# Last-layer weights converted from doubles beside the products that precede their use, earlier splits for the first expert, and four smaller edits

## The chip, the cores and the metric

One core of one Trainium2 chip runs the kernel. The metric is device time in microseconds (us), the median of the runs shown. Engines are named as in the profile: PE (TensorE matmul), PEld (its weight loads), DVE (VectorE), ACT (ScalarE), POOL (GpSimd) and SP (SyncE, which issues most DMAs). Lines such as L298 are lines of the kernel before.

## The reference

Three layers in a row, all in float32 at the ends: linear attention with a normalised output, a mixture of experts with one expert per token and a capacity, and a maxout layer.

```python
kv = einsum('bhsd,bhse->bhde', k, v); out = einsum('bhsd,bhde->bhse', q, kv)      # B 4, H 8, S 576, D 64
x = (out / sqrt(mean(out * out, -1) + 1e-6) * g_norm) as (2304, 512)
expert = argmax(x @ w_gate); gate = softmax weight of that expert                 # 8 experts
y[i] = gate * (relu(x[i] @ w1[e]) @ w2[e])       # w1 512x1024, w2 1024x512, first `capacity` tokens of each
h = maximum(maximum(y @ m1, y @ m2), y @ m3); result = h @ w_out                  # m 512x768, w_out 768x512
```

The four matrices of the maxout layer (`m1`, `m2`, `m3`, `w_out`) arrive as 64-bit doubles; everything else is 32-bit.

## The kernel before

**Stages.** The attention runs batch by batch (four of them). Each batch's tokens are normalised, routed and scattered to DRAM by expert; the tokens of the fullest expert are also picked straight from SBUF for the first expert's product. Eight experts follow (`r` from 0 to 7, the order ranked by load), then the maxout layer in six blocks of 384 tokens (`j` from 0 to 5).

**Splits.** Each big product is made of three passes in a rounded format: the operands are split into a high and a low part, and high x high, high x low and low x high are summed (`mm3`, L765 to L767). A weight tile of 128x512 therefore costs two instructions: the high part on ACT (L297) and the low part on DVE (L298). `split_next` does the next tile of one fixed stream: 16 tiles for each expert, then 18 of the three maxout matrices, then 6 of `w_out`. It is fed by `raw` tiles in a ring of four, loaded by SP (`raw_dma`), each reused when its two splits are done. Activations are split the same way: `h` (L788 on ACT, L789 on DVE), `xt` (L678, L679), `g` (L1099, L1100).

**An expert.** `gemm1_f` runs eight times (`f`), each giving 128 rows of `h`; `gemm2_dc` runs four times (`dc`) and reads all eight `h`. Between them the written order puts splits, gathers, the next expert's transposes and `dbl_step`s.

**Doubles.** `dbl_step` turns one 128x256 piece of a double matrix into float32: SP loads it, ACT rounds its two words (L912, L913), DVE does three integer steps (L914, L915, L917), POOL multiplies and adds (L918, L919), and ACT's queue stores the piece to DRAM. There are 48 pieces (36 of the three matrices, 12 of `w_out`), placed in experts 1 to 7 by the tables `DBL1` (after which `f`) and `DBL2` (how many after each `dc`).

**Maxout.** For each of six column blocks `c`, PE makes three products `pa` (12 groups of `mm3`, one bank of PSUM each). ACT copies the first (L1096), DVE takes the maximum with the second and the third (L1097, L1098), ACT and DVE split the result (L1099, L1100). Then three output tiles `pz` sum over the six blocks (L1109 to L1111). PSUM has six banks here (`psb`, bufs=6): block `c+2` writes over the banks of block `c`.

**Order.** Nothing reorders the program: each engine executes its queue in the order in which the program is written (`manual_schedule`), and waits at the head of the queue hold all that stands behind.

Of the kernel before, what the change touches and what calls it, by code (L numbers as in the profile page):

```python
# [40 lines left out]
def kernel(  # L41
# [21 lines left out]
    ct = dram.tile([NT, 3], F32, name="ct")  # L63

    doubles = []
    if m2w1.dtype == mybir.dt.int64:
        d64 = [m2w1, m2w2, m2w3, m2wo]
        m2w1, m2w2, m2w3 = (dram.tile([DM, F2], F32, name=f"m2w{a}") for a in range(3))
        m2wo = dram.tile([F2, DM], F32, name="m2wo")
        for cb in range(F2 // 256):  # L70
            for a, dst in enumerate([m2w1, m2w2, m2w3]):
                for rb in range(NDC):
                    doubles.append((d64[a], dst, rb, cb))
        for rb in range(NC2):
            for cb in range(DM // 256):
                doubles.append((d64[3], m2wo, rb, cb))
    ND = len(doubles)
# [155 lines left out]
    sp, act = ENG.SP, ENG.Activation  # L233
    NRAW = NE * 8 + 12
    NW = 20
# [12 lines left out]
    def raw_dma(i):  # L248
# [16 lines left out]
        if j < 9:  # L265
# [3 lines left out]
        j -= 9  # L269
        return nc.sync.dma_start(raw.rearrange("p (c f) -> p c f", c=2),  # L270
                                 m2wo[j * 256:(j + 1) * 256, :].rearrange("(c p) f -> p c f", p=128))

# [7 lines left out]

    def split_next(n=1, eng=None):
        for _ in range(n):
            i, half = divmod(stream[0], 2)
            stream[0] += 1
            if i >= NRAW:
                continue
            raw = raws[i]
            t_ = wtile(2 * i + half)
            wt[2 * i + half] = t_
            if i < NE * 8 + 9:  # L290
                src = raw.rearrange("p (c f) -> p c f", c=4)[:, :, half * 128:(half + 1) * 128]
                hi, lo = t_[:, 0], t_[:, 1]
            else:
                src = raw[:, half * 512:(half + 1) * 512]
                hi = t_[:, 0].rearrange("p c f -> p (c f)")
                lo = t_[:, 1].rearrange("p c f -> p (c f)")
            nc.scalar.activation(out=hi, in_=src, func=AF.Copy)  # L297
            (eng or nc.vector).tensor_tensor(out=lo, in0=src, in1=hi.bitcast(F32), op=ALU.subtract)  # L298
            if half == 1:
                raw_upto(i + 5)  # L300
# [101 lines left out]
    def out_rest(b, qT):  # L402
        po = ps_o.tile([128, 512], F32, tag="po", name=f"po{b}r")[:, 0:4 * LW].rearrange("p (j c) -> p j c", c=LW)
        sq = sa.tile([128, H, 2, D], F32, tag="sq", bufs=2, name=f"sq{b}r")[:, 0:2].rearrange("p a b d -> p (a b) d")
# [58 lines left out]
    def stats_steps(b, t0, t1, r_):  # L463
# [9 lines left out]
        yield  # L473
        nc.scalar.activation(out=sr, in_=ms, func=AF.Sqrt)
        yield
# [426 lines left out]
    def dbl_round(i):  # L902

        if i < ND:
            t_ = dt_[i]
            w_ = dpool[0].tile([128, 256], F32, tag="dw", bufs=6, name=f"dw{i}")
            dt_[i, "w"] = w_
            lo, hi = t_[:, :, 0], t_[:, :, 1]  # L910
            wi = w_.bitcast(I32)
            nc.scalar.activation(out=w_, in_=hi.bitcast(F32), func=AF.Copy, scale=2.0 ** -112)  # L912
            nc.scalar.activation(out=lo.bitcast(F32), in_=lo.bitcast(U32), func=AF.Copy, scale=2.0 ** -52)  # L913
            nc.vector.tensor_scalar(out=wi, in0=wi, scalar1=3, scalar2=None, op0=ALU.logical_shift_left)  # L914
            nc.vector.scalar_tensor_tensor(out=wi, in0=hi, scalar=-2 ** 31, in1=wi,  # L915
                                           op0=ALU.bitwise_and, op1=ALU.bitwise_or)
            nc.vector.tensor_scalar(out=hi, in0=wi, scalar1=-2 ** 23, scalar2=None, op0=ALU.bitwise_and)  # L917
            nc.gpsimd.tensor_tensor(out=lo.bitcast(F32), in0=hi.bitcast(F32), in1=lo.bitcast(F32), op=ALU.mult)  # L918
            nc.gpsimd.tensor_tensor(out=w_, in0=lo.bitcast(F32), in1=w_, op=ALU.add)  # L919

# [107 lines left out]

    DBL1 = [(), (3, 5), (3, 5), (1, 3, 5), (1, 4), (1, 4), (1, 4), (1, 3, 5, 7)]
    DBL2 = [(0, 0, 0, 0), (1, 1, 1, 2), (1, 2, 1, 2), (1, 2, 1, 2), (1, 1, 1, 2)] + [(1, 1, 1, 1)] * 2 + [(2, 2, 0, 0)]  # L1030
    for r in range(NE):
# [10 lines left out]
        if r == NE - 1:  # L1042
            ct_load()
        for f in range(NFC):
            gemm1_f(r, f)
            if r == 0:
                for _ in range(9 if f == 0 else 6):
                    next(rk_gen, None)
                if f == 3:
# [32 lines left out]
    for j in range(NYB):  # L1082
        h2 = []
        for c in range(NC2):
# [36 lines left out]
    with tc.If(flag):  # L1121
        spill(ctx, tc, dict(
            er_f=er_f, nr_f=nr_f, mr_f=mr_f, trir=trir, capf=capf, e2304=e2304, slot=slot, ident=ident, g2=g2,
            xs=xs, ct=ct, w1=w1, w2=w2, m2w=m2w, m2wo=m2wo, out=out))


def spill(ctx, tc, a):
# [3 lines left out]
    with ExitStack() as st:  # L1131
# [164 lines left out]
```

## Time and profile before

| what | value |
|---|---|
| median of 3 runs | 647.64 us (646.8 to 650.21) |
| the profiled execution, its own time | 650.49 us |
| its span | 648.6 us, granted clock 0.982 |
| PE busy | 619.0 us, 95% |
| DVE, ACT, POOL busy | 338.0, 274.0, 196.5 us |

The span runs from the first to the last profiled instruction; 1.9 us of the execution's own time lie around it. Attention lasts to about 88 us, the experts to about 337, the maxout layer to the end.

### The profile page before, as it was taken

How to read it: one execution, taken by the hardware profiler on the slowest of the kernel's cores; microseconds unless marked ns; L12 is line 12 of the kernel's file. 1: busy time of each engine (PE TensorE's matmuls, PEld its weight loads, DVE VectorE, ACT ScalarE, POOL GpSimd, SP SyncE). 2: the span in 40 equal slices, each digit the busy share in tenths (PEclk: the TensorE clock that was granted, in tenths of full speed). 3: DMA queues.
4: the chain of work that ended last, by engine and by line, in shares of the span. 5: the costliest groups of instructions: out<-in, count | busy, mean ns of one | idle time of the engine just before them, and what ended most of it. 6: DMA issues, size and time to landing. Idle time of an engine off the chain costs nothing.

```text
span 648.6 us, 11278 instructions
## 1 busy us (share of the span) xinstructions
PE 619.0 (95%) x4113; PEld 593.8 (92%) x4113; DVE 338.0 (52%) x718; ACT 274.0 (42%) x629; POOL 196.5 (30%) x278
## 2 busy tenths in 40 slices
PE   8898988999999999999999999999999999999992
PEld 8788888999998989999999989989989989989992
DVE  2546867886889888888985322222322222221220
ACT  1655864856575857576753221121121121121110
POOL 3247643122858585857530010010010010001001
PEclk9978998999999999999999999999999999999997
DMA  8999347866888788888962000000000000000000
GB/s 226 282 297 297 122 164 236 256 234 214 246 249 276 235 264 254 259 251 255 275 184 65 1 34 16 1 33 17 1 33 17 0 17 33 0 17 33 1 18 35
DMA packets 81373, 88.35 MB, mean 136 GB/s; under 512 B 15017, under 2 KB 70825, under 8 KB 81314
## 3 DMA queue, kind: packets, MB, share of 16 engines
q1 hardware_dynamic: 68448, 66.64, 35.5%
q0 software_dynamic: 5952, 14.65, 6.5%
q10 hardware_dynamic: 6914, 6.30, 2.8%
q8 instruction: 34, 0.56, 0.4%
q14 instruction: 25, 0.20, 0.1%
HBM read 71.80 MB, written 15.76 MB: 135 GB/s over the span
## 4 chain that ended last, share of the span: by engine, by line
PE 63%; DVE 9%; DMA 4%; issue 3%; ACT 2%; ACTq 0%; POOL 0%; SPq 0%; DVEq 0%; POOLq 0%
PE pa L767 12%; PE pa L766 12%; PE pa L765 12%; PE py L766 4%; DVE w L298 4%; PE py L767 4%; PE py L765 4%; PE pz L1110 4%; PE pz L1109 4%; PE pz L1111 4%; DVE h L789 2%; DMA d<-in_moe_w_dram 2%; PE ph L767 2%; PE ph L766 2%; PE ph L765 2%
## 5 line engine op out<-in xcount | busy, mean ns | idle before, releaser
L766 PE MATMUL pa<-ys,w 128*128 128x384 f32 x432 | 144.3, 334 | 0.0
L765 PE MATMUL pa<-ys,w 128*128 128x384 f32 x432 | 144.3, 334 | 0.0
L767 PE MATMUL pa<-ys,w 128*128 128x384 f32 x432 | 144.3, 334 | 0.0
L298 DVE TENSOR_TENSOR w<-raw,w 128x512 fp32r<-128x512 f32 x152 | 114.6, 783 | 26.7 <-ACT w L297 23.1
L1114 POOL DMA_INDIRECT out_dram<-o,ctab x18 | 17.5, 973 | 286.9 <-ACT o L1113 276.7
L1097 DVE TENSOR_TENSOR m<-pa,m 128x384 f32<-128x384 f32 x36 | 20.1, 558 | 137.6 <-PE pa L767 137.6
L297 ACT ACTIVATE w<-raw 128x512 fp32r<-128x512 f32 x152 | 89.5, 624 | 4.8 <-DMA raw<-in_moe_w_dram 4.8
L766 PE MATMUL py<-h,w 128*128 128x324 f32 (+7 forms) x256 | 81.4, 318 | 7.2 <-DVE h L789 7.2
L1099 ACT ACTIVATE g<-m 128x384 fp32r<-128x384 f32 x36 | 18.9, 526 | 150.0 <-DVE m L1098 150.0
L766 PEld LDWEIGHTS pa<-ys,w 128*128 128x128 f32 x432 | 81.1, 188 | 0.2
L765 PEld LDWEIGHTS pa<-ys,w 128*128 128x128 f32 x432 | 81.1, 188 | 0.2
L767 PEld LDWEIGHTS pa<-ys,w 128*128 128x128 f32 x432 | 81.1, 188 | 0.0
L765 PE MATMUL py<-h,w 128*128 128x324 f32 (+7 forms) x256 | 80.2, 313 | 0.0
L767 PE MATMUL ph<-xt,w 128*128 128x324 f32 (+7 forms) x256 | 79.6, 311 | 0.5 <-DVE w L298 0.5
L765 PE MATMUL ph<-xt,w 128*128 128x324 f32 (+7 forms) x256 | 79.3, 310 | 0.6 <-ACT xt L667 0.6
L767 PE MATMUL py<-h,w 128*128 128x324 f32 (+7 forms) x256 | 79.8, 312 | 0.0
L766 PE MATMUL ph<-xt,w 128*128 128x324 f32 (+7 forms) x256 | 79.4, 310 | 0.2 <-DVE xt L668 0.2
L766 PEld LDWEIGHTS py<-h,w 128*128 128x128 f32 x256 | 48.8, 191 | 10.8 <-DVE h L789 10.6
L918 POOL TENSOR_TENSOR d<-d 128x256 f32<-128x256 f32 x48 | 30.7, 640 | 75.5 <-issue 18.2
L765 PEld LDWEIGHTS ph<-xt,w 128*128 128x128 f32 x256 | 48.3, 189 | 0.8 <-ACT xt L667 0.8
L767 PEld LDWEIGHTS ph<-xt,w 128*128 128x128 f32 x256 | 48.3, 189 | 0.8 <-DVE w L298 0.8
L765 PEld LDWEIGHTS py<-h,w 128*128 128x128 f32 x256 | 48.9, 191 | 0.0
(247 smaller groups left out, 1034.1 us busy)
## 6 DMA issues: line engine op xcount, KB each, us to landing
raw<-in_moe_w_dram SPq DMA_DIRECT2D x64, 512.0 KB, 5.4
d<-in_moe_w_dram SPq DMA_DIRECT2D x36, 256.0 KB, 5.2
m2w<-dw ACTq DMA_DIRECT2D x36, 128.0 KB, 4.5
raw<-m2w SPq DMA_DIRECT2D x9, 512.0 KB, 4.6
k<-in_k_dram SPq DMA_DIRECT2D x8, 512.0 KB, 8.7
v<-in_v_dram SPq DMA_DIRECT2D x8, 512.0 KB, 9.2
q<-in_q_dram SPq DMA_DIRECT2D x8, 512.0 KB, 8.5
d<-in_moe_w_out_dram SPq DMA_DIRECT2D x12, 256.0 KB, 5.2
```

Source lines behind the costliest of these rows:

```text
L297: nc.scalar.activation(out=hi, in_=src, func=AF.Copy)
L298: (eng or nc.vector).tensor_tensor(out=lo, in0=src, in1=hi.bitcast(F32), op=ALU.subtract)
L765: nc.tensor.matmul(po, lhi, rhi, start=first, stop=False)
L766: nc.tensor.matmul(po, lhi, rlo, start=False, stop=False)
L767: nc.tensor.matmul(po, llo, rhi, start=False, stop=last)
L918: nc.gpsimd.tensor_tensor(out=lo.bitcast(F32), in0=hi.bitcast(F32), in1=lo.bitcast(F32), op=ALU.mult)
L1097: nc.vector.tensor_tensor(out=m_, in0=pa[1][:, :YB], in1=m_, op=ALU.max)
L1099: nc.scalar.activation(out=t_[:, 0], in_=m_, func=AF.Copy)
L1109: nc.tensor.matmul(po, h_[:, 0], w_[:, 0], start=c == 0, stop=False)
L1110: nc.tensor.matmul(po, h_[:, 0], w_[:, 1], start=False, stop=False)
L1111: nc.tensor.matmul(po, h_[:, 1], w_[:, 0], start=False, stop=c == NC2 - 1)
L1114: nc.gpsimd.indirect_dma_start(out=out, out_offset=IndirectOffsetOnAxis(ap=ctab[:, jt, 0:1].bitcast(I32), axis=0), in_=o_, in_offset=None)
```

## The change

- The 12 `w_out` pieces leave the `dbl_step` tables. Instead six 128x512 pieces of doubles are loaded as `raw` tiles and converted by the same seven operations (now a function, `to_float32`) inside `split_next`, in the first block of the maxout layer. The converted piece is split as before, and both parts are stored to DRAM for a fallback path that this input does not take.
- `DBL1` and `DBL2` spread the remaining 36 pieces anew.
- In expert 0 the splits stand ahead of the products: four before the first, two before each of the next four, one after each of the last two.
- The root of the sums of squares is taken on ACT from the sums themselves (scale and bias inside the instruction).
- In the last batch DVE scales three of five row sets instead of two, and does so ahead of the positions' cast; ACT scales two instead of three; one group of 128x128 products that keep PE busy is three long instead of four.
- A work tile of the rest rows gets a buffer of its own.

```diff
-    NRAW = NE * 8 + 12
+    NRAW = NE * 8 + 9 + NC2
...
-        return nc.sync.dma_start(raw.rearrange("p (c f) -> p c f", c=2),
-                                 m2wo[j * 256:(j + 1) * 256, :].rearrange("(c p) f -> p c f", p=128))
+        return nc.sync.dma_start(raw.bitcast(I32), m2wo[j * 128:(j + 1) * 128, :].bitcast(I32))
...
+    def to_float32(lo, hi, w_):
+        wi = w_.bitcast(I32)
+        nc.scalar.activation(out=w_, in_=hi.bitcast(F32), func=AF.Copy, scale=2.0 ** -112)
+        nc.scalar.activation(out=lo.bitcast(F32), in_=lo.bitcast(U32), func=AF.Copy, scale=2.0 ** -52)
+        nc.vector.tensor_scalar(out=wi, in0=wi, scalar1=3, scalar2=None, op0=ALU.logical_shift_left)
+        nc.vector.scalar_tensor_tensor(out=wi, in0=hi, scalar=-2 ** 31, in1=wi,
+                                       op0=ALU.bitwise_and, op1=ALU.bitwise_or)
+        nc.vector.tensor_scalar(out=hi, in0=wi, scalar1=-2 ** 23, scalar2=None, op0=ALU.bitwise_and)
+        nc.gpsimd.tensor_tensor(out=lo.bitcast(F32), in0=hi.bitcast(F32), in1=lo.bitcast(F32), op=ALU.mult)
+        nc.gpsimd.tensor_tensor(out=w_, in0=lo.bitcast(F32), in1=w_, op=ALU.add)
...
             else:
-                src = raw[:, half * 512:(half + 1) * 512]
...
+                src = xgs[0].tile([128, H, D], F32, tag="xn", name=f"wd{i}").rearrange("p h d -> p (h d)")
+                words = raw.bitcast(I32).rearrange("p (f c) -> p f c", c=2)
+                to_float32(words[:, :, 0], words[:, :, 1], src)
             nc.scalar.activation(out=hi, in_=src, func=AF.Copy)
...
+            if i >= NE * 8 + 9:
+                c0 = (i - NE * 8 - 9) * 128
+                nc.sync.dma_start(m2wos[c0:c0 + 128].rearrange("p s f -> p (s f)"),
+                                  t_.bitcast(F32).rearrange("p s c f -> p (s c f)"))
...
-        nc.scalar.activation(out=sr, in_=ms, func=AF.Sqrt)
+        nc.scalar.activation(out=sr, in_=s_, func=AF.Sqrt, scale=1.0 / D, bias=eps)
...
-    for s in SORD[:3]:
+    for s in SORD[:2]:
         normalise(b, s, nc.scalar)
-    keep_warm(ps_o.tile([128, 512], F32, tag="po", name="warm6"), 4)
+    keep_warm(ps_o.tile([128, 512], F32, tag="po", name="warm6"), 3)
...
     own(b)
+    for s in SORD[2:]:
+        normalise(b, s, nc.vector)
     send(b)
-    for s in SORD[3:]:
-        normalise(b, s, nc.vector)
...
-    DBL1 = [(), (3, 5), (3, 5), (1, 3, 5), (1, 4), (1, 4), (1, 4), (1, 3, 5, 7)]
-    DBL2 = [(0, 0, 0, 0), (1, 1, 1, 2), (1, 2, 1, 2), (1, 2, 1, 2), (1, 1, 1, 2)] + [(1, 1, 1, 1)] * 2 + [(2, 2, 0, 0)]
+    DBL1 = [(), (3, 5, 7), (1, 3, 5, 7), (1, 3, 5, 7), (3, 7), (7,), (), (1, 3, 5)]
+    DBL2 = [(0,) * 4] + [(1,) * 4] * 3 + [(1,) * 4, (1, 1, 1, 0), (1, 1, 1, 0), (0,) * 4]
...
         for f in range(NFC):
+            if r == 0:
+                split_next(4 if f == 0 else 2 if f < 5 else 0)
             gemm1_f(r, f)
...
-            split_next(1 if r else 2 if f < 6 else 0)
+            split_next(1 if r or f > 5 else 0)
...
             if j == 0:
-                split_next(2)
+                split_next(2 if c < 2 else 1)
```

**ACT in the first maxout block, column blocks 1 to 3.** Before (`raw` to `w` is a split; `m`, `g` the maximum and its split):

```order
L1099 ACTIVATE g_4865<-m_4864 128x384
L297 ACTIVATE w_4910<-raw_4734 128x512
L297 ACTIVATE w_4913<-raw_4734 128x512
L1096 ACTIVATE m_4916<-pa_4871 128x384
L1099 ACTIVATE g_4917<-m_4916 128x384
L297 ACTIVATE w_4962<-raw_4779 128x512
L297 ACTIVATE w_4965<-raw_4779 128x512
L1096 ACTIVATE m_4968<-pa_4923 128x384
```

Of the change (`wd` is the float32 that DVE and POOL complete; the L312 row reads it):

```order
L1110 ACTIVATE g_4729<-m_4728 128x384
L283 ACTIVATE wd_4775<-raw_4598 128x512
L284 ACTIVATE raw_4598<-raw_4598 128x512
L312 ACTIVATE w_4774<-wd_4775 128x512
L283 ACTIVATE wd_4789<-raw_4641 128x512
L284 ACTIVATE raw_4641<-raw_4641 128x512
L312 ACTIVATE w_4788<-wd_4789 128x512
L1107 ACTIVATE m_4802<-pa_4735 128x384
L1110 ACTIVATE g_4803<-m_4802 128x384
L283 ACTIVATE wd_4849<-raw_4675 128x512
L284 ACTIVATE raw_4675<-raw_4675 128x512
L312 ACTIVATE w_4848<-wd_4849 128x512
```

Two conversions now stand between the `g` of block 0 and the `m` of block 1, and one ahead of the `m` of each later block.

**DVE in expert 0, up to the first `h`.** Before, and then of the change:

```order
L1023 CAST po_i<-po_f 128x4
L789 SCALAR_TENSOR_TENSOR h_1369<-ph_1356,h_1369 128x324
L808 COPY cnt<-pc 128x8
L811 SCALAR_TENSOR_TENSOR key<-cnt,key_199 128x8
L813 TENSOR_TENSOR gt<-key 128x64
```

```order
L1032 CAST po_i<-po_f 128x4
L313 TENSOR_TENSOR w_1350<-raw_701,w_1350 128x512
L313 TENSOR_TENSOR w_1353<-raw_701,w_1353 128x512
L313 TENSOR_TENSOR w_1358<-raw_703,w_1358 128x512
L313 TENSOR_TENSOR w_1361<-raw_703,w_1361 128x512
L810 SCALAR_TENSOR_TENSOR h_1379<-ph_1366,h_1379 128x324
```

Four splits moved ahead of the first `h`; what stood between later `h` moved up with them.

**DVE in expert 7, around the last two `h`.** Before, and then of the change:

```order
L914 TENSOR_SCALAR dw_4601<-dw_4601 128x256
L915 SCALAR_TENSOR_TENSOR dw_4601<-d_4436,dw_4601 128x256
L917 TENSOR_SCALAR d_4436<-dw_4601 128x256
L789 SCALAR_TENSOR_TENSOR h_4622<-ph_4609,h_4622 128x284
L298 TENSOR_TENSOR w_4625<-raw_4433,w_4625 128x512
L789 SCALAR_TENSOR_TENSOR h_4641<-ph_4628,h_4641 128x284
```

```order
L313 TENSOR_TENSOR w_4486<-raw_4312,w_4486 128x512
L810 SCALAR_TENSOR_TENSOR h_4505<-ph_4492,h_4505 128x284
L313 TENSOR_TENSOR w_4508<-raw_4355,w_4508 128x512
L810 SCALAR_TENSOR_TENSOR h_4524<-ph_4511,h_4524 128x284
```

The rounds of doubles between the `h` are gone there.

## Rows read from the trace of the kernel before

**Rows 1.** The page, part 1: busy time of each engine.

```profile
PE 619.0 (95%) x4113; PEld 593.8 (92%) x4113; DVE 338.0 (52%) x718; ACT 274.0 (42%) x629; POOL 196.5 (30%) x278
```

**Rows 2.** Page and lines by form: all experts, expert 0, expert 3 (busy, mean | idle before).

```profile
L766 PE MATMUL py<-h,w 128*128 128x324 f32 (+7 forms) x256 | 81.4, 318 | 7.2 <-DVE h L789 7.2
...
L766 PE MATMUL py<-h,w 128*128 128x324 f32 x32 | 10.9, 342 | 2.1 <-DVE h L789 2.1
...
L766 PE MATMUL py<-h,w 128*128 128x330 f32 x32 | 10.2, 319 | 1.6 <-DVE h L789 1.6
```

**Rows 3.** Windows: start:end, length, busy of the engines, PEclk, DMA share, GB/s.

```profile
200.00:210.00 10.00, 8.45 (x55) 7.90 (x53) 9.72 (x19) 3.88 (x9) 8.97 (x11) 1.00 0.97 295
344.00:357.00 13.00, 13.00 (x77) 13.00 (x76) 6.00 (x11) 4.35 (x9) 0.00 (x0) 1.00 0.03 11
```

**Rows 4.** Timeline of DVE, maxout block 0 (start, us, instruction, idle before).

```profile
349.78 0.56 DVE L1098 TENSOR_TENSOR m<-pa,m 128x384 f32<-128x384 f32 x1 [1.45 <-PE pa L767]
350.94 0.56 DVE L1100 TENSOR_TENSOR g<-m,g 128x384 fp32r<-128x384 f32 x1 [0.59 <-ACT g L1099]
...
356.02 0.56 DVE L1098 TENSOR_TENSOR m<-pa,m 128x384 f32<-128x384 f32 x1 [1.45 <-PE pa L767]
```

**Rows 5.** Timeline of ACT, maxout block 0.

```profile
344.13 0.53 ACT L1099 ACTIVATE g<-m 128x384 fp32r<-128x384 f32 x1 [2.72 <-DVE m L1098]
344.56 1.14 ACT L297 ACTIVATE w<-raw 128x512 fp32r<-128x512 f32 x2
345.62 0.49 ACT L1096 ACTIVATE m<-pa 128x384 f32<-128x384 f32 x1
350.38 0.53 ACT L1099 ACTIVATE g<-m 128x384 fp32r<-128x384 f32 x1 [4.26 <-DVE m L1098]
```

**Rows 6.** Timeline of DVE, a split and one round of doubles in expert 2.

```profile
159.90 0.69 DVE L298 TENSOR_TENSOR w<-raw,w 128x512 fp32r<-128x512 f32 x1
160.50 0.29 DVE L914 TENSOR_SCALAR dw<-dw 128x256 int32<-128x256 int32 x1
...
161.56 0.29 DVE L914 TENSOR_SCALAR dw<-dw 128x256 int32<-128x256 int32 x1
```

**Rows 7.** Timeline of POOL: one round's second operation, and a whole round.

```profile
304.30 1.09 POOL L919 TENSOR_TENSOR dw<-d,dw 128x256 f32<-128x256 f32 x1
...
307.13 0.61 POOL L918 TENSOR_TENSOR d<-d 128x256 f32<-128x256 f32 x1 [1.75 <-ACT xt L678]
307.82 0.75 POOL L919 TENSOR_TENSOR dw<-d,dw 128x256 f32<-128x256 f32 x1
```

**Rows 8.** Lines by form: a scaling of 512 columns in attention, on POOL.

```profile
L516 POOL TENSOR_TENSOR orow<-ohl,rnorm 128x512 f32<-128x512 f32 x12 | 12.1, 1033 | 0.0
```

**Rows 9.** Timeline of PE, maxout block 0: the first output tile's sixteenth product.

```profile
378.03 0.40 PE L1109 MATMUL pz<-w,g 128*128 128x512 f32 x1
```

**Rows 10.** Timeline of PE in expert 0, around its two waits.

```profile
107.81 0.42 PE L766 MATMUL py<-h,w 128*128 128x324 f32 x1 [1.16 <-DVE h L789]
...
109.42 0.54 PE L766 MATMUL py<-h,w 128*128 128x324 f32 x1 [0.90 <-DVE h L789]
...
110.29 0.47 PE L766 MATMUL py<-h,w 128*128 128x324 f32 x1
```

**Rows 11.** Windows: the stretch after those waits.

```profile
109.00:113.00 4.00, 3.58 (x14) 3.58 (x15) 0.77 (x2) 1.35 (x5) 0.00 (x0) 0.57 0.88 260
```

**Rows 12.** Timeline of DVE in expert 0: the first and the last `h`.

```profile
93.90 0.50 DVE L789 SCALAR_TENSOR_TENSOR h<-ph,h 128x324 fp32r<-128x324 f32 x1 [2.59 <-ACT h L788]
...
108.88 0.89 DVE L789 SCALAR_TENSOR_TENSOR h<-ph,h 128x324 fp32r<-128x324 f32 x2
```

**Rows 13.** Timeline of PE, end of attention: dummies, routing.

```profile
79.88 1.09 PE L331 MATMUL warm<-ident 128*128 128x128 f32 x8
80.81 0.18 PE L531 MATMUL pp<-ohsum,ones 128*128 128x40 bf16 x1
```

More of the change, by code (lines that the diff above doesn't have):

```diff
@@ L66 @@
     if m2w1.dtype == mybir.dt.int64:
-        d64 = [m2w1, m2w2, m2w3, m2wo]
+        d64 = [m2w1, m2w2, m2w3]
         m2w1, m2w2, m2w3 = (dram.tile([DM, F2], F32, name=f"m2w{a}") for a in range(3))
-        m2wo = dram.tile([F2, DM], F32, name="m2wo")
+        m2wos = dram.tile([F2, 2, DM], F32, name="m2wos")
         for cb in range(F2 // 256):
@@ L73 @@
                     doubles.append((d64[a], dst, rb, cb))
-        for rb in range(NC2):
-            for cb in range(DM // 256):
-                doubles.append((d64[3], m2wo, rb, cb))
     ND = len(doubles)
@@ L279, in raw_upto, with split_next @@
             issued[0] += 1
-    def split_next(n=1, eng=None):
+    def to_float32(lo, hi, w_):
[8 more added lines that the diff above has]
+        nc.gpsimd.tensor_tensor(out=w_, in0=lo.bitcast(F32), in1=w_, op=ALU.add)
+    def split_next(n=1):
         for _ in range(n):
-            i, half = divmod(stream[0], 2)
+            t = stream[0]
             stream[0] += 1
-            if i >= NRAW:
+            if t >= NT1 + 18 + NC2:
                 continue
+            i = t // 2 if t < NT1 + 18 else NE * 8 + 9 + t - NT1 - 18
             raw = raws[i]
-            t_ = wtile(2 * i + half)
-            wt[2 * i + half] = t_
+            t_ = wtile(t)
+            wt[t] = t_
             if i < NE * 8 + 9:
+                half = t % 2
                 src = raw.rearrange("p (c f) -> p c f", c=4)[:, :, half * 128:(half + 1) * 128]
@@ L293, in split_next @@
             else:
-                src = raw[:, half * 512:(half + 1) * 512]
-                hi = t_[:, 0].rearrange("p c f -> p (c f)")
-                lo = t_[:, 1].rearrange("p c f -> p (c f)")
-            nc.scalar.activation(out=hi, in_=src, func=AF.Copy)
-            (eng or nc.vector).tensor_tensor(out=lo, in0=src, in1=hi.bitcast(F32), op=ALU.subtract)
+                half = 1
+                hi, lo = (t_[:, x].rearrange("p c f -> p (c f)") for x in range(2))
+                src = xgs[0].tile([128, H, D], F32, tag="xn", name=f"wd{i}").rearrange("p h d -> p (h d)")
+                words = raw.bitcast(I32).rearrange("p (f c) -> p f c", c=2)
+                to_float32(words[:, :, 0], words[:, :, 1], src)
+            nc.scalar.activation(out=hi, in_=src, func=AF.Copy)
+            nc.vector.tensor_tensor(out=lo, in0=src, in1=hi.bitcast(F32), op=ALU.subtract)
+            if i >= NE * 8 + 9:
+                c0 = (i - NE * 8 - 9) * 128
+                nc.sync.dma_start(m2wos[c0:c0 + 128].rearrange("p s f -> p (s f)"),
+                                  t_.bitcast(F32).rearrange("p s c f -> p (s c f)"))
             if half == 1:
@@ L322 @@
         nc.vector.memset(ss[i][D:128, 0, :], 1.0)
+    eps = sl_.tile([128, 1], F32, name="eps")
+    nc.vector.memset(eps, EPS)
     ohsum = sl_.tile([128, B + 1, NE], BF16, name="ohsum")
@@ L403, in out_rest @@
         po = ps_o.tile([128, 512], F32, tag="po", name=f"po{b}r")[:, 0:4 * LW].rearrange("p (j c) -> p j c", c=LW)
-        sq = sa.tile([128, H, 2, D], F32, tag="sq", bufs=2, name=f"sq{b}r")[:, 0:2].rearrange("p a b d -> p (a b) d")
+        sq = sa.tile([128, 4, D], F32, tag="sqr", bufs=1, name=f"sq{b}r")
         for h in range(H):
@@ L909, in dbl_round @@
             dt_[i, "w"] = w_
[L910 to L919, printed above, removed]
+            to_float32(t_[:, :, 0], t_[:, :, 1], w_)
     def dbl_store(i):
@@ L1123 @@
             er_f=er_f, nr_f=nr_f, mr_f=mr_f, trir=trir, capf=capf, e2304=e2304, slot=slot, ident=ident, g2=g2,
-            xs=xs, ct=ct, w1=w1, w2=w2, m2w=m2w, m2wo=m2wo, out=out))
+            xs=xs, ct=ct, w1=w1, w2=w2, m2w=m2w, m2wos=m2wos, out=out))
 def spill(ctx, tc, a):
@@ L1191, in spill @@
         wo = wpool.tile([128, NC2, DM], F32, name="sp_wo")
-        nc.sync.dma_start(wo, a["m2wo"].rearrange("(c p) f -> p c f", p=128))
+        wl = wpool.tile([128, NC2, DM], F32, name="sp_wl")
+        for i, w_ in enumerate((wo, wl)):
+            nc.sync.dma_start(w_, a["m2wos"].rearrange("(c p) s f -> s p c f", p=128)[i])
+        V.tensor_tensor(out=wo, in0=wo, in1=wl, op=ALU.add)
         def ps(nm):
```

## The prediction

> **What bounds the kernel now.** I read the page's busy times first: PE is busy 95% of the span, 619.0 of 648.6 us, and no other engine is near it [rows 1]. So the product stream is the path, and a change can win only what PE loses. Next, where it loses it. The grouped waits of PE on the second layer's products name DVE's low half of `h`, 7.2 us in all: 2.1 in expert 0, 5.1 in experts 1 to 7, none of them with more than expert 3's 1.6 [rows 2]. The windows tell why: around expert 3's waits DVE is busy 9.72 of 10 us and POOL 8.97 [rows 3]. DVE carries the weight splits, the `h` and the rounds of doubles, and falls behind. In the maxout layer it is the other way round: in 344 to 357 us PE is busy all 13 us, DVE 6.00, ACT 4.35, POOL nothing [rows 3]. That idle room is where the change puts the last quarter of the doubles.
>
> But an average share does not say whether work fits. What has to be read there is the period. One column block takes PE 6.24 us, from 349.78 to 356.02 [rows 4]. PE has banks for two blocks, so it may start block `c+2` only when ACT has copied the first product of block `c`. Today ACT does that 1.06 us after it began two splits, with no wait in between [rows 5].
>
> **The change, part by part.**
>
> *Conversions in maxout block 0.* The order on ACT shows that between `g` of one block and `m` of the next now stands a conversion whose last ACT instruction (the high half) waits for POOL, which waits for DVE, which waits for ACT. ACT's queue is in order, so the copy that frees PE's bank waits behind all of it. One period of that loop is: `g` on ACT 0.53 [rows 5]; its low half on DVE 0.56 [rows 4]; three integer steps on DVE; two operations on POOL; the high half on ACT, 0.6 (a pair takes 1.14) [rows 5]; the low half on DVE 0.65, between the 0.69 and the 0.60 to the next start [rows 6]; two maxima on DVE, 2 x 0.56 [rows 4]; six handovers of some 0.05, 0.3.
>
> The two unknowns are the wide operations. DVE's three steps take 1.06 us for 256 columns, from 160.50 to 161.56 [rows 6]. For 512 they lie between that (the width costs nothing) and 2.12; I take the middle, 1.6, because each has a fixed part. POOL's pair takes 0.61 + 0.08 + 0.75 = 1.44 when it runs undisturbed and 0.61 + 0.08 + 1.09 = 1.78 beside a busy DVE [rows 7]. Doubled that is some 2.8 to 3.4 (one gap of 0.08 in each); one 512-wide product on POOL takes 1.03 [rows 8], so two take at least 2.06. I take 2.6: undisturbed, since DVE waits in this loop, and a little under double. The period is then 0.53 + 0.56 + 1.6 + 2.6 + 0.6 + 0.65 + 1.12 + 0.3 = 8.0 us against PE's 6.24. Bounds: 6.9 with 1.06 and 2.06, and 9.3 with 2.12 and 3.4.
>
> The Trainium skill (GPSIMD Engine Reference, 3.1 Elementwise) gives some 2.6 cycles an element for a two-input operation; at 1.2 GHz an estimate of 1.1 us for 512, 2.2 for the pair and 7.6 for the period. The trace's 0.75 for 256 is already above half of that page's figure, so I stay with the rows.
>
> Now the sequence. `g` of block 0 begins at 344.13 [rows 5]. The first conversion has its high half 0.53 + 0.56 + 1.6 + 2.6 + 0.6 + 0.25 = 6.1 us later, its low half 0.65 after that, 350.9. Block 1 carries two: the second adds 1.6 + 2.6 + 0.6 + 0.65 + 0.2 = 5.7, so 356.6, then two maxima, and `g` of block 1 begins at 357.75 (today 350.38). Four more periods of 8.0 put `g` of block 5 at 389.75, its high half at 390.3. The first output tile needs that at its sixteenth product, which today runs at 378.03 [rows 9]. The first product of block 5 in that tile thus comes **12.2 us late**: about 1.7 at each of three blocks, and the rest in one wait inside the first output tile. Nothing later gives it back, PE being the path from there. With the lower bounds the same sum is 5 us, with the upper ones 20.
>
> *The clock after that wait.* In expert 0, two waits of 1.16 and 0.90 within some 3 us [rows 10] were followed by 4 us at a mean granted clock of 0.57 [rows 11], so most of them at the lower level (1.2 GHz) where PE otherwise has 2.4. That cost 4 x (1 - 0.57) = 1.7 us. A wait of 6 us should do the same once: **+1.5**, between 0 and 3.
>
> *Experts 1 to 7.* 12 of 48 rounds leave; each takes 1.06 us of DVE [rows 6], 1.4 to 1.8 of POOL [rows 7]. By the new tables experts 4 to 7 have two, two, two and three rounds fewer ahead of the last `h`: 2 to 3 us, more than any of them waits today (all under expert 3's 1.6), so those waits go. Expert 1 begins with two splits less behind it. Experts 2 and 3 keep as many rounds in all (8 and 8 for 8 and 9), one of them earlier: I leave 0.5 of expert 3's 1.6 and 0.2 elsewhere. **-4.4** of 5.1; bounds 0 and -5.1. What is late next there is nothing: PE then runs product to product. The 12 loads and 12 stores that leave also ease a DMA share of 0.97 [rows 3]; I cost that at nothing, since the waits it causes are among the 5.1.
>
> *Expert 0.* DVE runs without a gap from the first `h` at 93.90 to the end of the last at 109.77 [rows 12]. That is 15.9 us of splits, `h` and ranking, and all of it must precede the last `h` in the new order as well, plus one more split. The splits begin when the first `h` did, because ACT is held to that time by the register loads of the placement. So the last `h` comes at about 93.8 + 15.9 + 0.6 = 110.3; the product that needs it runs at 110.29 today [rows 10]. **0**, bounds -1.5 and +1.5: earlier splits only move the wait to other `h`.
>
> *End of attention.* Eight passes of dummies take 1.09, and the routing follows at 80.81 [rows 13]; one group of four is now three, a quarter less: -0.27. The root no longer waits for the sum's scaling, but ACT reaches it at the same time behind its copies: -0.05. The third set on DVE takes 0.69 and is wanted only by the third of five groups of the last pick: 0. **-0.3**, 0 to -0.7. The queues passed over: SP gets six loads and six stores of 512 KB in place of 12 loads of 256 KB and three of 512, when nothing else waits on SP; POOL's scatters of the output stand behind the conversions and follow PE anyway: 0.
>
> Sum: 12.2 + 1.5 - 4.4 + 0 - 0.3 = +9.0. The profiled execution took 650.49 us and would take 659.5; it lies 2.85 above the median of the runs shown, 647.64, so the forecast is **656.6 us** for the median.
>
> **The rivals.**
>
> *The conversions hide (faster, chance 0.11).* Their place is the same loop. If the wide operations cost little more than narrow ones (1.06 and 1.44), the period is 0.53 + 0.56 + 1.06 + 1.44 + 0.6 + 0.65 + 1.12 + 0.3 = 6.3, PE keeps its pace, and only the last block is late: `g` of block 5 at 379.5, 2.0 us. With -5.1 in the experts, -0.3 and no low clock: -3.4, or 644.2. For it speaks the idle room [rows 3]; against it POOL's 1.03 for one wide product [rows 8]. Where the period falls below about 6.8 the change breaks even.
>
> *Every wait costs clock (slower still, 0.15).* The small waits of the first three late blocks may each bring the low clock that one pair of waits brought in expert 0 [rows 11]: three times 1.5 more, 661.1. Against: expert 3 lost 1.6 us in one place [rows 2] and the window around it is granted 1.00 throughout [rows 3]. By the Trainium skill (TensorE: Matmul & The Clock Gate, A second HAM failure mode), waits on PSUM between groups of products made another kernel's clock swing between its two levels; expert 3 does not bear that out here.
>
> *The experts keep their waits (slower, 0.14).* If raw loads or the splits themselves hold DVE back and not the rounds of doubles, 5.1 us stay: 656.6 + 4.4 = 661.0. For it: the DMA share of 0.97 [rows 3]. Against: experts 5 to 7 lose a quarter or more of what DVE does ahead of their last `h`.
>
> **How the numbers follow.** My forecast holds 0.60. The range reaches from 645.5 (most of the hidden case lies below, so under 0.1 is left out) to 664.0 (the two slower rivals with room; the upper bounds of POOL and DVE, +8 more, would lie above, another 0.08). About 0.5%, 3.2 us, is what a measurement can tell from no change here: under 644.4 is faster, above 650.9 slower. Faster: most of the hidden case, 0.09. Same: its rest and the forecast with its lower bounds (5 - 4.4), 0.11. Slower: 0.80.
>
> **What the profile would show.** Right: in the first maxout block the idle time of PE's `pa` products is put down to ACT's `m`, near 1.7 us at blocks 3, 4 and 5, and one wait of some 6 us stands in the first `pz`; ACT's wait before the high half of each `wd` is on POOL, about 4.5 us, six times; a stretch at half clock follows. In experts 4 to 7 no product waits for `h`. Wrong: `pa` products 0.17 apart without a gap through block 0, or POOL's pair under 1.5 us; or `h` waits still near 5 us.

## The result and the profile after

The change is slower: 650.69 us (median of 19 runs) against 648.04 us (19 runs of the kernel before beside them). The ratio is 1.0056, with a 95% interval of 1.0036 to 1.0076: +3.6 us, between +2.3 and +4.9. The forecast was +9.0. The prediction's own line for "slower" (0.5%, 3.2 us) lies inside that interval, so by its line the result is on the border of "same". The profiled execution took 649.34 us, its span is 647.5 us.

Three parts of the page of the change: the busy times (PE was 619.0 [rows 1]), the granted clock in 40 slices, and the groups of products with idle time before them.

```profile
PE 612.7 (95%) x4111; PEld 588.6 (91%) x4111; DVE 328.8 (51%) x702; ACT 271.5 (42%) x609; POOL 192.0 (30%) x266
...
PEclk9999998999999999999999979999999999999997
...
L786 PE MATMUL pa<-ys,w 128*128 128x384 f32 x432 | 144.7, 335 | 2.6 <-ACT m L1107 2.6
...
L787 PE MATMUL py<-h,w 128*128 128x324 f32 (+7 forms) x256 | 80.1, 313 | 2.6 <-DVE off_f L901 2.1
...
L1120 PE MATMUL pz<-w,g 128*128 128x512 f32 x108 | 43.6, 404 | 7.4 <-ACT g L1110 6.1
```

The second layer's products waited 7.2 us for `h` [rows 2]; now 2.6, all of it in expert 0 and put down to DVE's tiles of the placement. In their place stand waits that the kernel before did not have: `pa` on ACT's copy `m`, and `pz` on ACT's `g`.

Where the time went is read from the starts of the first product of each stage. (A second profile of the kernel before was taken, see the experiments.) What the expectations call attention's last transposition is the first product of `po3r` (L408), the rest rows of the last batch.

| from the first product of ... to that of the next, us | before, two profiles | the change | difference |
|---|---|---|---|
| start to `po3r` | 71.84, 65.32 | 66.18 | inside the spread |
| then to expert 0 | 16.42, 16.42 | 16.20 | -0.22 |
| expert 0 | 35.43, 35.38 | 35.22 | -0.2 |
| expert 1 | 34.30, 34.07 | 33.62 | -0.7, -0.5 |
| expert 2 | 31.91, 31.91 | 31.91 | 0 |
| expert 3 | 32.46, 32.44 | 30.61 | -1.8 |
| expert 4 | 31.00, 31.00 | 28.92 | -2.1 |
| expert 5 | 29.36, 29.38 | 27.65 | -1.7 |
| experts 6 and 7 | 54.35, 54.33 | 52.39 | -2.0 |
| maxout block 0 | 49.99, 50.01 | 63.31 | **+13.3** |
| from block 1 to the last block's first `pz` | 237.36, 237.36 | 237.36 | 0 |

From expert 2 on, two profiles of one kernel agree within 0.02 us in each row, so this table tells more than the medians, which carry the spread of attention. It sums to +4.6 or +4.9, beside +3.6 (2.3 to 4.9) measured.

**Maxout block 0: as forecast.** The timeline of ACT (start, us, instruction, idle before), then of DVE and of POOL in the same period:

```profile
343.07 0.53 ACT L1110 ACTIVATE g<-m 128x384 fp32r<-128x384 f32 x1 [1.51 <-DVE m L1109]
343.50 0.65 ACT L283 ACTIVATE wd<-raw 128x512 f32<-128x512 f32 x1
344.06 0.67 ACT L284 ACTIVATE raw<-raw 128x512 f32<-128x512 uint32 x1
348.38 0.63 ACT L312 ACTIVATE w<-wd 128x512 fp32r<-128x512 f32 x1 [3.65 <-POOL wd L290]
348.91 0.47 ACT L1107 ACTIVATE m<-pa 128x384 f32<-128x384 f32 x1
350.89 0.53 ACT L1110 ACTIVATE g<-m 128x384 fp32r<-128x384 f32 x1 [1.51 <-DVE m L1109]
```

```profile
344.18 0.43 DVE L285 TENSOR_SCALAR wd<-wd 128x512 int32<-128x512 int32 x1
344.64 0.69 DVE L286 SCALAR_TENSOR_TENSOR wd<-raw,wd 128x512 int32<-128x512 int32 x1
345.37 0.43 DVE L288 TENSOR_SCALAR raw<-wd 128x512 int32<-128x512 int32 x1
349.04 0.69 DVE L313 TENSOR_TENSOR w<-wd,w 128x512 fp32r<-128x512 f32 x1 [3.24 <-ACT w L312]
```

```profile
345.93 1.04 POOL L289 TENSOR_TENSOR raw<-raw 128x512 f32<-128x512 f32 x1 [5.42 <-DVE raw L288]
347.05 1.30 POOL L290 TENSOR_TENSOR wd<-raw,wd 128x512 f32<-128x512 f32 x1
```

From `g` to `g` it is now 7.82 us (6.25 in [rows 5]). Every engine waits in turn: DVE 1.62 us, POOL 2.42, the high half on ACT, the low half on DVE. ACT stands 3.65 us in front of the high half, and the `m` behind it, which frees PE's bank, stands with it. What that does to PE, in its timeline:

```profile
349.44 0.44 PE L786 MATMUL pa<-ys,w 128*128 128x384 f32 x1 [1.30 <-ACT m L1107]
...
374.98 0.80 PE L1120 MATMUL pz<-w,g 128*128 128x512 f32 x1 [6.10 <-ACT g L1110]
375.57 0.63 PE L1121 MATMUL pz<-w,g 128*128 128x512 f32 x1
376.00 0.63 PE L1122 MATMUL pz<-w,g 128*128 128x512 f32 x1
...
379.29 0.39 PE L1121 MATMUL pz<-w,g 128*128 128x512 f32 x1
```

The wait at 349.44 comes three times (at 357.28 again, and at 365.12 ahead of the first `pz`), then the long one, inside the first output tile. After it nine products start 0.42 to 0.59 us after the one before, where 0.23 is usual.

### The profile page after: what moved, and what is told of

Same layout as the page of the kernel before. It is cut to its first block, busy times and chain, and to the rows that moved or that the text cites. A ratio compares the mean times of both kernels' runs of the same rounds, so it can differ in the third digit from the quotient of the medians.

```text
span 647.5 us, 11168 instructions
## 1 busy us (share of the span) xinstructions
PE 612.7 (95%) x4111; PEld 588.6 (91%) x4111; DVE 328.8 (51%) x702; ACT 271.5 (42%) x609; POOL 192.0 (30%) x266
## 3 DMA queue, kind: packets, MB, share of 16 engines
q1 hardware_dynamic: 67632, 68.21, 35.8%
## 5 line engine op out<-in xcount | busy, mean ns | idle before, releaser
L313 DVE TENSOR_TENSOR w<-raw,w 128x512 fp32r<-128x512 f32 x146 | 107.8, 765 | 33.6 <-ACT w L312 30.6
L312 ACT ACTIVATE w<-raw 128x512 fp32r<-128x512 f32 x146 | 86.1, 623 | 5.8 <-issue 3.8
L1120 PE MATMUL pz<-w,g 128*128 128x512 f32 x108 | 43.6, 404 | 7.4 <-ACT g L1110 6.1
```

The source lines that it names most:

```text
L313: nc.vector.tensor_tensor(out=lo, in0=src, in1=hi.bitcast(F32), op=ALU.subtract)
L1120: nc.tensor.matmul(po, h_[:, 0], w_[:, 0], start=c == 0, stop=False)
```

## The experiments

Totals are against the kernel before, run beside each on the same chip. Stage times are as in the table above.

**Front and late weights apart.** The first kernel is the change without its smaller parts (its diff against the change is below, cut), the second the kernel before with the front alone, the third the kernel before with the early splits alone.

```diff
-            if r == 0:
-                split_next(4 if f == 0 else 2 if f < 5 else 0)
...
-            split_next(1 if r or f > 5 else 0)
+            split_next(1 if r else 2 if f < 6 else 0)
...
-        nc.scalar.activation(out=sr, in_=s_, func=AF.Sqrt, scale=1.0 / D, bias=eps)
+        nc.scalar.activation(out=sr, in_=ms, func=AF.Sqrt)
...
-    keep_warm(ps_o.tile([128, 512], F32, tag="po", name="warm6"), 3)
+    keep_warm(ps_o.tile([128, 512], F32, tag="po", name="warm6"), 4)
```

> The change with its smaller parts undone: roots, dummies, the third VectorE set and the early splits of expert 0 as before; only the new tables and the output weights' conversion in the maxout layer stay. My theory (only these two move the time): 0 to +0.5 us against the change, so about +4 us against the kernel before; in the maxout loop the period of g on ScalarE stays 7.8 us and no product of experts 1 to 7 waits for h. Rival (the front's edits give the 5 us that the two traces differ by before the experts): about +9 us against the kernel before.

Measured: 652.94 us, ratio 1.011 (1.007 to 1.0149), +7.1 us (4.5 to 9.7). That lies between the two expectations, so the total settles nothing. The stages do. No 5 us come from the front: `po3r` starts at 66.4 us, and at 66.2 in the change. Experts 3 to 7 take 139.7 (139.6 in the change). The excess sits in expert 1, 35.8 for 33.6; ahead of expert 0, 18.4 for 16.2, where the clock was granted 0.58 from 80 to 92 us; and in maxout block 0, 64.2 for 63.3, where twelve products and not eight start 0.43 us apart after the long wait. Expert 0 gives 2.0 back. (Expert 1 is the late splits', see the last experiment; the low clock ahead of expert 0 comes and goes with the execution, see the third kernel.) My "no product of experts 1 to 7 waits for h" was wrong for expert 1.

> The kernel before with the end-of-attention edits alone (roots from the sums, 3 dummies for 8, the third set on VectorE). My theory: -0.2 us, between the last transposition of attention and the first product of expert 0, and nothing that can be measured otherwise (same). Rival (the 5 us by which the two traces differ in attention come from these edits): -4 to -5 us.

Measured: 646.13 us, ratio 0.9984 (0.9952 to 1.0017), -1.0 us (-3.1 to +1.1): nothing that can be told from no change, and the stretch ahead of expert 0 is 16.20 for 16.42, the -0.22 of the change. The rival falls.

> The kernel before with the splits ahead of the first expert's products alone. My theory (an earlier split only moves the waits of expert 0 to other h): 0, between -1.5 and +1.5 us, and the waits on h in expert 0 no less than the kernel before's 2.1 us. Rival (the change's front is worth about 2 us more than the late weights alone, and this edit is where): -1.5 to -3 us.

Measured: 646.01 us, ratio 0.9957 (0.9923 to 0.999), -2.8 us (-5.0 to -0.6). That is outside my band and in the rival's. The waits on `h` listed in expert 0 are 1.2 us, and not 2.1 or more as I expected. In its own profile experts 0 and 1 take 68.4 us, where the two profiles of before have 69.7 and 69.4. From `po3r` to expert 2 it takes 87.7 all the same, for 86.2 and 85.9, since the stretch ahead of expert 0 is 19.3 for 16.4, with the clock granted 0.57 from 80 to 92 us. Three other profiles show such a stretch, one with the splits as before and two with the early ones, and one of the two profiles of the piped kernel shows it while the other does not: it is no work of this edit. So 1.0 to 1.3 of the 2.8 can be the splits'; the rest is left open (see the last experiment).

**Attention's 5 us.**

> The kernel before once more, for a second profile of it. If the 5 us between the two profiles in attention are no work of the edits: attention's last transposition begins up to 5 us earlier than in the first profile, at a higher granted clock in 26 to 72 us, while the waits on h in the experts and the maxout layer stay the same. If they are: the first profile's times return within 1 us.

Measured: 643.6 us (one run), and `po3r` at 65.32 where it was at 71.84. The windows of the first profile of before and then of the second (start:end, length, busy of the engines, PEclk, DMA share, GB/s):

```profile
26.00:50.00 24.00, 20.66 (x246) 18.61 (x247) 14.55 (x43) 13.04 (x32) 11.70 (x16) 0.79 1.03 298
```

```profile
26.00:50.00 24.00, 19.30 (x274) 16.91 (x270) 18.53 (x54) 15.30 (x38) 16.08 (x20) 1.00 1.06 311
```

Same kernel, clock 0.79 and 1.00, 28 products more in the second. Over 14 profiles of 12 kernels `po3r` starts between 64.3 and 71.8 us. One kernel alone varies by more than the 5.7 us by which the first two traces differ there, so I do not put these down to the edits, and I leave attention out of the account.

**ScalarE's wait taken off the copy.** The end of each conversion (high half, low half, store; `finish`) is issued one column block later. The first conversion also starts one block earlier, so that block 1 carries one and not two:

```diff
             if j == 0:
-                split_next(2 if c < 2 else 1)
+                finish()
+                split_next(3 if c == 0 else 1)
...
+        if j == 0:
+            finish()
```

> The change with the last steps of each conversion in the maxout layer (high half, low half, store) issued one column block later, so that ScalarE's copy of a product no longer stands behind a wait for GpSimd; the arithmetic is the same. My theory (the loss is the in-order wait on ScalarE, the gain is the 12 rounds taken from the experts): the maxout period falls from 7.83 to PE's 6.24 us, the long wait in the first output tile goes, the experts stay as in the change; about 13 us less than the change, -8 to -9 us against the kernel before (near 639.5 us). Rival (VectorE and GpSimd together have no room for the conversions there, whatever the order): the period stays above 7 us and the time within 4 us of the change's.

> The piped kernel once more, for a narrower interval and beside the one without the early splits: 636 to 639 us; from expert 2 to the end every stage within 0.1 us of its first profile, attention anywhere within 4 us of it.

Measured: 636.34 us, ratio 0.9844 (0.9804 to 0.9884), -10.1 us (-12.7 to -7.5), and the second time 636.87 us, 0.9832 (0.9794 to 0.9869). This version beats both kernels. Maxout block 0 takes 49.98 us, as before the change, with the change's instructions in it. Its ACT timeline:

```profile
343.82 0.53 ACT L1122 ACTIVATE g<-m 128x384 fp32r<-128x384 f32 x1 [3.68 <-DVE m L1121]
344.26 0.62 ACT L325 ACTIVATE w<-wd 128x512 fp32r<-128x512 f32 x1
344.78 0.66 ACT L283 ACTIVATE wd<-raw 128x512 f32<-128x512 f32 x1
345.90 0.48 ACT L1119 ACTIVATE m<-pa 128x384 f32<-128x384 f32 x1
350.07 0.53 ACT L1122 ACTIVATE g<-m 128x384 fp32r<-128x384 f32 x1 [3.68 <-DVE m L1121]
```

The period is 6.25 us, the high half (L325) waits for nothing, and `m` runs 2.1 us after `g` (5.8 in the change). So there was room, and the order alone decided whether it was used. (What the earlier start of one conversion adds to this was not run apart; the next experiment shows that block 1's second conversion delays its `g`.) Stage by stage the second profile repeats the first from expert 2 on; before that it differs by 3.3 us: expert 0 began late and at a mean clock of 0.77 (84 to 100 us).

**The period as a sum.** GpSimd's pair goes to VectorE, the order stays:

```diff
-        nc.gpsimd.tensor_tensor(out=lo.bitcast(F32), in0=hi.bitcast(F32), in1=lo.bitcast(F32), op=ALU.mult)
-        nc.gpsimd.tensor_tensor(out=w_, in0=lo.bitcast(F32), in1=w_, op=ALU.add)
+        nc.vector.tensor_tensor(out=lo.bitcast(F32), in0=hi.bitcast(F32), in1=lo.bitcast(F32), op=ALU.mult)
+        nc.vector.tensor_tensor(out=w_, in0=lo.bitcast(F32), in1=w_, op=ALU.add)
```

> The change with the wide multiply and add of the maxout layer's conversions on VectorE and not on GpSimd; the order is the same. My theory (the period is a sum of steps in a row): the pair of 1.04 + 1.30 = 2.34 us and a handover of 0.1 become about 1.1 us, the period falls by 1.2 to 1.4 to 6.4 to 6.6 us, nearly PE's 6.24, and the block's late end shrinks from 13.3 to 3 to 5 us; 4 to 5 us less than the kernel before. Rival (the wait of ScalarE in itself costs a fixed time at each block, whatever stands ahead of it): the period stays near 7.8 and the time near the change's.

Measured: 644.32 us, ratio 0.9966 (0.9937 to 0.9995), -2.2 us (-4.1 to -0.3). DVE in one period:

```profile
345.61 0.43 DVE L288 TENSOR_SCALAR raw<-wd 128x512 int32<-128x512 int32 x1
346.15 0.69 DVE L289 TENSOR_TENSOR raw<-raw 128x512 f32<-128x512 f32 x1
346.88 0.69 DVE L290 TENSOR_TENSOR wd<-raw,wd 128x512 f32<-128x512 f32 x1
```

The three integer steps end at 346.04, the pair at 347.57: 1.53 us, where POOL needs 2.55 from the same point (345.80 to 348.35). 1.02 less gives 6.80, and the period measured is 6.82 (343.30 to 350.19 and on to 357.01 are 6.89 and 6.82). The period is the sum of its steps; I had priced the pair at 1.1. Block 0 loses 7.1 us and not 3 to 5. The second conversion of block 1, which I left out of that expectation, holds `g` of block 1 back by 5.0 (18.30 us after the maxout layer's first product, 13.27 in the piped kernel), and four periods of 0.58 too many are 2.3 more. Of these, 2.1 are slack: the sixteenth product of the first output tile comes 5.3 late, in one wait of 5.10 idle. The other 1.8 are the low clock behind that wait, granted 0.51 from 368 to 375 us.

**What made the experts wait.** Both kernels are the piped one plus the tables of before, in which the last 12 steps (end of expert 5, experts 6 and 7) either only move data or only compute, the latter on one spare tile. Of the diffs, these are the tables, which both have, and the lines of the traffic:

```diff
-    DBL1 = [(), (3, 5, 7), (1, 3, 5, 7), (1, 3, 5, 7), (3, 7), (7,), (), (1, 3, 5)]
+    DBL1 = [(), (3, 5), (3, 5), (1, 3, 5), (1, 4), (1, 4), (1, 4), (1, 3, 5, 7)]
...
+            nc.sync.dma_start(t_, m2wo[rb * 128:(rb + 1) * 128, cb * 256:(cb + 1) * 256].bitcast(I32))
...
+            nc.scalar.dma_start(spare[i - 3 - ND], xt_[i - 3][:, 0:256])
```

> The change with the conversion's end one block later, and added to it the kernel before's 12 loads and 12 stores of doubles in the experts, moving data with no conversion behind them. If the traffic of those steps made the products of experts 1 to 7 wait for h: the 8 us that the change gained there come back, near 645 us. If VectorE's and GpSimd's rounds did: the experts stay as in the piped kernel, near 636 us, and no product of experts 1 to 7 waits for h.

> The change with the conversion's end one block later, and added to it the kernel before's 12 rounds of doubles in the experts, computed on a tile that is never loaded or stored, at the steps where the kernel before has them. If the rounds themselves make products wait for h: waits on h of 4 to 5 us by the idle time before them in experts 1 to 7, expert 3 first with about 1.6, and about 8 us more than the piped kernel, near 644 us. If the traffic did: near 636 us.

Measured: traffic 643.36 us, ratio 0.9923 (0.9893 to 0.9953); rounds 641.9 us, 0.9913 (0.9874 to 0.9952). By the totals each brings back more than half of the experts' gain, which neither theory allows. The experts tell why:

| us | piped | traffic | rounds | no GpSimd | GpSimd only | before |
|---|---|---|---|---|---|---|
| expert 3 | 30.61 | 32.71 | 31.47 | 31.71 | 31.69 | 32.46 |
| expert 4 | 28.92 | 30.68 | 30.88 | 30.67 | 30.64 | 31.00 |
| expert 5 | 27.64 | 29.30 | 29.10 | 29.10 | 29.04 | 29.36 |
| experts 6, 7 | 52.39 | 52.39 | 54.30 | 52.39 | 52.39 | 54.35 |

The edit changed one thing more than it was meant to: with the old tables, the 36 rounds that remain stand in experts 1 to 5 as densely as before, and there the waits are, but for expert 3's longest, those of before in every column. Only experts 6 and 7 separate the two. There the traffic costs nothing, with no product waiting for `h`; the rounds without traffic cost 1.91 us, nearly all that the kernel before loses there (1.96). So there the rounds did it. In experts 3 to 5 the new tables both thin the rounds out and spread them, with their loads and stores, and no run takes these apart. (Expert 3's longest wait, 1.06 in the traffic kernel, is absent in the three with rounds; they have five work buffers for six, and I did not follow that up.)

The next two split those added rounds. The first leaves GpSimd's pair out of them (its call is below), the second keeps that pair alone:

```diff
-                       dpool[0].tile([128, 256], F32, tag="dw", bufs=5, name=f"dxw{i}"))
+                       dpool[0].tile([128, 256], F32, tag="dw", bufs=5, name=f"dxw{i}"), pool=False)
```

> The kernel with the 12 added rounds, but the added rounds (they stand in experts 6 and 7 and at the end of 5) do only their ScalarE and VectorE steps, not GpSimd's pair. In experts 6 and 7 the full rounds cost 1.9 us against the piped kernel (54.30 for 52.39 from expert 6 to the maxout layer). If VectorE's own 1.06 us a round delays h: nearly all of it stays, 1.5 us or more. If GpSimd's pair does, by stretching VectorE's instructions beside it: under 0.7 us stays.

> The same kernel with only GpSimd's pair in the 12 added rounds, no ScalarE or VectorE step. If VectorE's own steps delay h: experts 6 and 7 take within 0.4 us of the piped kernel's 52.39, no product waits for h there. If the stretching of VectorE's instructions beside GpSimd's does: at least half of the 1.9 us stays.

Measured: 643.07 us, ratio 0.9931 (0.9896 to 0.9967), and 640.78 us, 0.9883 (0.9837 to 0.9929). In experts 6 and 7 both take 52.39 us, and no product waits for `h`: neither half alone holds `h` back, only both together. Both theories fall, since each wanted one half to do it. What both halves share is VectorE's time: its own steps, and the lengthening of its instructions beside GpSimd's (last section). DVE's timeline in expert 7 bears that out, first of the kernel with whole rounds, then without GpSimd's pair (from one `h` to the second after it):

```profile
309.11 0.45 DVE L821 SCALAR_TENSOR_TENSOR h<-ph,h 128x284 fp32r<-128x284 f32 x1
309.48 1.03 DVE L315 TENSOR_TENSOR w<-raw,w 128x512 fp32r<-128x512 f32 x1
...
312.64 0.45 DVE L821 SCALAR_TENSOR_TENSOR h<-ph,h 128x284 fp32r<-128x284 f32 x1
```

```profile
307.08 0.45 DVE L823 SCALAR_TENSOR_TENSOR h<-ph,h 128x284 fp32r<-128x284 f32 x1
307.45 0.68 DVE L317 TENSOR_TENSOR w<-raw,w 128x512 fp32r<-128x512 f32 x1
...
310.00 0.45 DVE L823 SCALAR_TENSOR_TENSOR h<-ph,h 128x284 fp32r<-128x284 f32 x1
```

PE gives two rows of products `ph` in 3.20 us there. The same seven VectorE instructions (two `h`, two splits, three steps of a round) take 3.53 us beside GpSimd's pair (3.52 in the kernel before, from 318.30 to 321.82) and 2.92 without it. The three steps are 1.05 of the 3.53, so the lengthened rest alone would take an estimated 2.5. Only with both does VectorE fall behind PE: its last `h` begins 16.5 us into expert 7, and 13.4 in the two kernels with half the rounds and in the piped one. (With GpSimd's pair alone the pairs wait for nothing on VectorE and run earlier, up to 8 us into expert 7, so that kernel does not test them beside the last `h`.)

**Early splits, once more.**

> The piped kernel with the splits of expert 0 again behind its products, as in the kernel before. My theory of the prediction (earlier splits only move the wait): within 1 us of the piped kernel. Rival (the late splits leave a backlog for which expert 1 waits): 1 to 3 us slower than the piped kernel, with waits on h in expert 1 and more time from its second layer to expert 2 than 17.5 us.

Measured: 637.23 us, ratio 0.9827 (0.9792 to 0.9863), beside 636.87 and 0.9832 for the piped kernel on the same chip: no difference that the totals can tell. Expert 1 does wait, as the rival has it (1.28 and 0.52 us on `h`, 20.2 us from its second layer to expert 2), and takes 37.3 us for 33.8 and 34.8; expert 0 is shorter, 33.7 for 35.4 and 35.6. In these profiles 0.7 to 1.9 us stay from expert 0 to expert 2 (71.0 for 69.2 and 70.3), too little for the medians. Over all profiles these two experts take 68.2 to 70.3 us in the nine with the early splits (mean 69.1) and 69.0 to 72.1 in the five without (mean 70.3). So the splits mostly move the wait from one expert to the other; they may be worth about 1 us, which the two totals (0.4 us here, 2.8 above) do not settle.

## Why the prediction was right and wrong

*Conversions in maxout block 0, +12.2: held.* Period 7.83 (8.0), POOL's pair 1.04 + 1.30 (2.6), DVE's steps 1.6 (1.6), three waits of 1.3 idle and one of 6.1. The sixteenth product of the first output tile comes 11.3 late (12.2). With the clock it was to be 13.7; it is 13.3. The estimate from the Trainium skill (GPSIMD Engine Reference, 3.1 Elementwise) for the pair was 2.2; the measured 2.34 lies between that and my 2.6.

*The clock after the long wait, +1.5: held, 2.0.* From 374.98 to 379.29 ten products start where 2.3 us would do, 4.3. Windows of the change, while PE stood (from 368.9) and after:

```profile
371.00:372.00 1.00, 0.00 (x0) 0.00 (x0) 0.00 (x0) 0.12 (x1) 0.85 (x1) 1.00 0.00 0
372.00:373.00 1.00, 0.00 (x0) 0.00 (x0) 0.46 (x1) 0.89 (x2) 0.00 (x0) 0.66 0.00 0
...
378.00:379.00 1.00, 1.00 (x4) 0.71 (x4) 0.00 (x0) 0.00 (x0) 0.70 (x1) 0.50 0.00 0
379.00:380.00 1.00, 1.00 (x6) 0.82 (x5) 0.00 (x0) 0.00 (x0) 0.00 (x0) 0.93 0.67 262
```

*The rival of a clock loss at every wait: wrong.* Around the three waits of 1.3 us the clock is granted 1.00 throughout (349 to 352, 357 to 360, 365 to 367). The rule of the Trainium skill that spoke for it (TensorE: Matmul & The Clock Gate, A second HAM failure mode) is not borne out by these waits.

*Experts 1 to 7, -4.4: this step failed.* The term was sized too small: the experts gained 8.0 to 8.3 us, more than my bound of -5.1. That the waits go was right, and that fewer rounds do it is what experts 6 and 7 show. The size was wrong in two ways. I left 0.7 us of waits, in expert 3 and elsewhere, that went too. There I counted the rounds of each expert alone; by the tables, 9 stand between the last `h` of expert 2 and that of expert 3 before and 8 after. (Expert 4 has one fewer ahead of its last `h`, two to one, and not two as I said.) And I took the idle time before a product [rows 2] for the loss. The kernel before, PE at the last two waits of expert 7:

```profile
325.21 0.30 PE L767 MATMUL py<-h,w 128*128 128x284 f32 x1
325.35 0.29 PE L765 MATMUL py<-h,w 128*128 128x284 f32 x1
325.83 0.40 PE L766 MATMUL py<-h,w 128*128 128x284 f32 x1 [0.19 <-DVE h L789]
326.07 0.29 PE L767 MATMUL py<-h,w 128*128 128x284 f32 x1
326.20 0.29 PE L765 MATMUL py<-h,w 128*128 128x284 f32 x1
327.13 0.40 PE L766 MATMUL py<-h,w 128*128 128x284 f32 x1 [0.64 <-DVE h L789]
327.37 0.29 PE L767 MATMUL py<-h,w 128*128 128x284 f32 x1
```

Without waits these products start 0.13 us apart though each is shown 0.29 long. At the first wait the starts are 0.48 and then 0.24 apart, so 0.35 + 0.11 are lost where 0.19 is listed; at the second 0.93 and 0.24, so 0.80 + 0.11 for 0.64. Together 1.37 for 0.83, and the stage is 1.34 longer than in the change (14.14 for 12.80 us from this layer's first product to the maxout layer). That is 0.27 more for each wait. The trace lists 11 waits in experts 1 to 7: carried over to all of them, 3.0 us, and with the 5.1 listed 8.1. Expert by expert this comes within 0.4 us of what the table of stages shows. It could have been read from the trace of before.

*Expert 0, 0, and the end of attention, -0.3: held* (-0.2 and -0.22). In expert 0 the wait moved, as I had it, though the 2.6 us are now listed behind small placement steps of DVE that stand beside its `h`. *The conversions hide* and *the experts keep their waits: both rivals wrong* for this kernel; the piped kernel shows that in another order the conversions do hide.

So direction and mechanism were right, a loss in the maxout layer over a smaller gain in the experts. Of the 5.4 us between +9.0 and +3.6, the experts' term explains 3.6 to 3.9, the maxout terms 0.4, expert 0 some 0.2; the rest, about 1, is inside the interval.

## What to carry to other kernels

Price a wait of PE from the distance between the starts of its products, not from the idle time that the view lists. Products overlap, so to the listed time come a product's length minus the usual distance between two starts, and the slower first product. A chain over three engines must not end in an in-order queue ahead of a copy that frees a bank; here, with its end issued one iteration later, the same work fits. Before believing an experiment's total, read its stages: here the kernels with the traffic and with the rounds alone have nearly equal totals, and only one of them loses time in experts 6 and 7.

## What the runs showed of the hardware

GpSimd's arithmetic lengthens some of VectorE's instructions beside it, here to 2.1 to 2.5 times their length. The kernel before around expert 3's waits, DVE and then POOL:

```profile
205.69 0.70 DVE L914 TENSOR_SCALAR dw<-dw 128x256 int32<-128x256 int32 x1
206.43 0.92 DVE L915 SCALAR_TENSOR_TENSOR dw<-d,dw 128x256 int32<-128x256 int32 x1
207.45 0.29 DVE L917 TENSOR_SCALAR d<-dw 128x256 int32<-128x256 int32 x1
207.66 0.49 DVE L789 SCALAR_TENSOR_TENSOR h<-ph,h 128x330 fp32r<-128x330 f32 x1
208.07 1.44 DVE L298 TENSOR_TENSOR w<-raw,w 128x512 fp32r<-128x512 f32 x1
```

```profile
205.18 1.06 POOL L918 TENSOR_TENSOR d<-d 128x256 f32<-128x256 f32 x1
206.32 0.75 POOL L919 TENSOR_TENSOR dw<-d,dw 128x256 f32<-128x256 f32 x1
207.23 1.04 POOL L1000 DMA_INDIRECT ct<-cto,ci_i  x1 [0.16 <-issue]
208.32 0.63 POOL L918 TENSOR_TENSOR d<-d 128x256 f32<-128x256 f32 x1
209.03 1.08 POOL L919 TENSOR_TENSOR dw<-d,dw 128x256 f32<-128x256 f32 x1
```

The split takes 1.44 us here and 0.69 in the maxout layer, where POOL rests; the second integer step (L915) 0.92, where 0.42 is its usual length, and the first (L914) 0.70 for 0.28. `h`, which reads PSUM and one SBUF tile, keeps its 0.49 (at 209.44 beside POOL's add too), and the steps beside POOL's indirect DMA (L917, 0.29) keep theirs. From 115 us to the maxout layer, the 122 splits of the kernel before have a mean of 0.81 us. By the Trainium skill (GPSIMD Engine Reference, 1. Specifications) GpSimd shares its SBUF interface with VectorE, with contention for VectorE's instructions that have two SBUF inputs or a two-port mode. The traces agree for those with two SBUF inputs (L298, L915) and for `h`; L914 has one, and whether it runs in such a mode no trace here tells. A round's 1.06 us on DVE [rows 6] is thus its price with POOL at rest: this one took 0.70, 0.92 and 0.29 us for its three steps.
